# Three small steps of every stage from VectorE to GpSimd, in a scheduled speech-codec encoder

## Chip, cores and metric

The kernel runs on one core of one Trainium2 chip. The metric is the device time of one execution in microseconds (us). Engines are named as in the profile: PE (TensorE), with PEld for its weight loads, DVE (VectorE), ACT (ScalarE), POOL (GpSimd), SP (SyncE, which here only issues DMAs).

## The reference

B = 2, T = 16000, D = 512; three taps, four stages (Nq) of eight codes (C) each; bf16 in and out.

```python
z = silu(sum_i xp[:, i:i+T, :] * dw_enc[i])        # depthwise filter, 3 taps
res, q = z, 0
for s in range(Nq):
    cb = codebooks[s]
    d2 = (res*res).sum(-1)[..., None] - 2 * res @ cb.T + (cb*cb).sum(-1)
    sel = cb[d2.argmin(-1)]
    q, res = q + sel, res - sel
y = sum_i qp[:, i:i+T, :] * dw_dec[i]              # depthwise filter, 3 taps
```

## The kernel before

The 32000 tokens are spread over 128 partitions, 250 positions each. The positions are cut into 16 chunks (`SIZES`: 12, then fourteen of 16, then 14). A chunk lies in SBUF with channels on the partitions, as four column blocks of 128 channels.

**Front of a chunk** (`load`, `front`). SP fetches the rows with transposing DMAs (L486, tile XT, two buffers). For each column block DVE makes three tap products (L553, tiles Z and T). They are added either on DVE (L561) or by an accumulating DMA that POOL issues (L559, Z<-T). The list `DMA_ADDS` says which: all four blocks of the first sum and one block of the second, from the second chunk on. ACT then does exp, log and exp (L565, L573, L576), DVE adds one in between (L569) and multiplies into the residual (L581, tile RES, three buffers).

**A stage** (`stage`, four per chunk). PE multiplies the residual with itself and with the code words into PSUM (L637, L643). DVE takes the diagonal out of it (L651, TR) and copies the dots (L654, PR). Then three small DVE steps over 16 x 8 numbers per partition: `with_norm` adds norm and dots (L673, V), `distance` adds the code norms and writes the upper half of a 32-bit word (L679, KEY), `ranks` writes the lower half (L684), so that ties go to the first code. DVE takes the minimum of the words (L689, M) and compares (L697, OH). PE transposes the one-hot rows (L707), and DVE copies them back (L714, OHT).

For stages 0 to 2 the residual is then updated, one instruction for two quarters of a column block. Either PE selects the code words (L731, SEL) and DVE adds them to RES (L747), or PE also multiplies the old residual by the identity (L752, NEW) and ACT writes the sum back (L758). `ON_DVE` gives the number of the four column blocks that go to DVE in stages 0, 1 and 2; chunk n takes entry n modulo the length, the last three chunks `ON_DVE_LAST`.

**Outputs** (`outputs`, `finish`). PE multiplies the one-hot rows with filtered code words (L785), ACT copies to SBUF (L791), SP stores (L795).

**Order.** All is put in order before the program is built. `Plan` holds a list of tasks with an engine, a hold, a delay and a due time; `run` makes passes forward and backward over it, with random shifts from the seeds in `ROUNDS`; the instructions are then emitted by start time. So each engine runs a fixed queue, with the work of up to three chunks mixed in it. A planned "DMA" engine stands for all DMAs. Its transposes and adds are of two kinds, and `APART` is a gap that the plan puts between kinds.

On the chip `keep_apart` adds a wait: with `LAG` n, each transposing DMA waits for the n-th last add before it in program order, and each add for the n-th last transpose. The adds stand in POOL's queue, transposes and stores in SP's.

Of the kernel before, what the change touches and what calls it, by code (L numbers as in the profile page):

```python
# [13 lines left out]
ALU = mybir.AluOpType  # L14
# [11 lines left out]
SIZES = [12] + [16] * 14 + [14]  # L26


ON_DVE = [(1, 2, 2)]
ON_DVE_LAST = [(2, 2, 2)]  # L30
LAST = 3

# [3 lines left out]

EARLY = 1

RUN = 4

AHEAD = 40
# [2 lines left out]
PERIOD, LEAD, STAGE, LATE, SPREAD = 56, 0.4, 0.9, 0.3, 0.3  # L44
FAR = -3.3e38

ROUNDS = [(940, 0.3, 0.0, 7), (4101, 0.3, 2.0, 9), (5991, 0.3, 0.0, 7), (15520, 0.3, 0.0, 10)]


CELLS, COLUMNS, ROWS = range(3)  # L50
WHOLE = (CELLS, CELLS, 0, 0.0)
SWITCH, CLING, SLOW = 0.1, 10.0, 1.08
RUNS, ADDS = (1, 1, 0, 0.0), (2, 2, 0, 0.0)
APART, CLUMP = 0.5, 2.0

LAG = 2


class Plan:
# [18 lines left out]
    def pass_over(self, rank, backward=False):  # L78

        tasks = self.tasks  # L80
        needs = [t[3] for t in tasks]
        after = [[] for _ in tasks]
        for n, ds in enumerate(needs):
            for d in ds:
                after[d].append(n)
        if backward:
            needs, after = after, needs
        takes, gives = (7, 6) if backward else (6, 7)
        left = [len(d) for d in needs]
        engines = list(dict.fromkeys(t[0] for t in tasks))  # L90
        ready = {e: [] for e in engines}
        until = {e: 0.0 for e in engines}
        slots = dict(self.slots)
        for n, t in enumerate(tasks):
            if not left[n]:
                heapq.heappush(ready[t[0]], (rank[n], n))
        now, events, order, starts, before = 0.0, [], [], [0.0] * len(tasks), WHOLE
        sort, ended = 0, 0.0
        while True:
            going = True  # L100
            while going:
                going = False
                for e in engines:
                    if until[e] > now + 1e-9:
                        continue
                    passed, pick, least, gap = [], None, 0.0, 0.0
                    while e == "DMA" and ready[e]:
                        at, n = heapq.heappop(ready[e])
                        passed.append((at, n))
                        if all(slots[k] > 0 for k in tasks[n][takes]):  # L110
                            kind, lost = tasks[n][8][0], 0.0
                            if kind and sort and kind != sort:
                                lost = max(0.0, APART - (now - ended))
                            if pick is None or at + CLUMP * lost < least:
                                pick, least, gap = n, at + CLUMP * lost, lost
                    while e == "PE" and ready[e]:
                        at, n = heapq.heappop(ready[e])
                        passed.append((at, n))
                        if all(slots[k] > 0 for k in tasks[n][takes]):
                            here = tasks[n][8]  # L120
                            lost = self.between(here, before) if backward else self.between(before, here)
                            if pick is None or at + CLING * lost < least:
                                pick, least, gap = n, at + CLING * lost, lost
                    if pick is not None:
                        passed = [v for v in passed if v[1] != pick]
                        if e == "PE":
                            before = tasks[pick][8]
                        elif tasks[pick][8][0]:
                            sort, ended = tasks[pick][8][0], now + gap + tasks[pick][1]
                    while pick is None and ready[e]:  # L130
                        at, n = heapq.heappop(ready[e])
                        if all(slots[k] > 0 for k in tasks[n][takes]):
                            pick = n
                            break
                        passed.append((at, n))
                    for p in passed:
                        heapq.heappush(ready[e], p)
                    if pick is None:
                        continue
                    t = tasks[pick]  # L140
                    for k in t[takes]:
                        slots[k] -= 1
                    order.append(pick)
                    starts[pick] = now
                    until[e] = now + gap + t[1]
                    heapq.heappush(events, (now + gap + t[1], -1))
                    heapq.heappush(events, (now + gap + max(t[1], t[2]), pick))
                    going = True
            if len(order) == len(tasks):
                return starts, order  # L150
            now = events[0][0]
            while events and events[0][0] <= now + 1e-9:
                _, n = heapq.heappop(events)
                if n < 0:
                    continue
                for k in tasks[n][gives]:
                    slots[k] += 1
                for a in after[n]:
                    left[a] -= 1
                    if not left[a]:  # L160
                        heapq.heappush(ready[tasks[a][0]], (rank[a], a))
# [46 lines left out]
def kernel(  # L208
# [8 lines left out]
    nc = tc.nc  # L217
    P = nc.NUM_PARTITIONS
# [254 lines left out]
    def load(st, org):  # L473
# [10 lines left out]
        def run(n, m):  # L484
            g = g0 + n - 1
            t = nc.sync.dma_start_transpose(out=st["XT"][:, n:n + m, :, :].rearrange("p n i t -> p (n i) t"),  # L486
                                        in_=xv[:, g:g + m, :].rearrange("p g d -> p (g d)"))
            keep_apart(t, runs, adds)
# [26 lines left out]
        for n in range(0, G + 2, RUN):  # L515
            due = org - 2.2 * PERIOD + 0.01 * n
            m = min(RUN, inside - n)
            if m > 0:
                done.append(plan.add("DMA", 0.7 * m, 2.7 + 0.7 * m, [room], due, lambda n=n, m=m: run(n, m), mode=RUNS))
        if inside < G + 2:  # L520
            t = plan.add("DMA", 0.9, 3.2, [room], due, lambda: edge(G + 1), mode=RUNS)
            st["edge"] = plan.add("POOL", 1.0, 1.4, [t], due, lambda: shift(G + 1))
# [91 lines left out]
    def stage(st, s, due):  # L614
# [55 lines left out]

        def with_norm():
            u["V"] = small.tile([P, GC, C], BF16, name="V")
            nc.vector.tensor_tensor(out=u["V"][:, 0:G, :], in0=u["PR"][:, 0:G, :], in1=u["TR"][:, 0:G].to_broadcast([P, G, C]),  # L673
                                    op=ALU.add)

        def distance():
            u["KEY"] = free["KEY"].pop(0)
            g2 = GPOS[:, C * s:C * s + C].rearrange("p (o c) -> p o c", o=1).to_broadcast([P, G, C])
            nc.vector.tensor_tensor(out=u["KEY"][1][:, 0:G, :, 1], in0=u["V"][:, 0:G, :], in1=g2, op=ALU.add)  # L679

        def ranks():

            word = u["KEY"][1]
            nc.vector.scalar_tensor_tensor(out=word[:, 0:G, :, 0], in0=word[:, 0:G, :, 1], scalar=0.0,  # L684
                                           in1=RANK.to_broadcast([P, G, C]), op0=ALU.is_lt, op1=ALU.subtract)

# [28 lines left out]
            st["OHT"] = u["OHT"]  # L715

        due += 0.01 * PERIOD
        t = plan.add("DVE", 0.2, 0.33, maxima, due, with_norm)
        t = plan.add("DVE", 0.2, 0.33, [t] + preset[0:3], due, distance, take=("KEY",))
        t = plan.add("DVE", 0.2, 0.33, [t], due, ranks)  # L720
        t = plan.add("DVE", 0.2, 0.33, [t], due, least)
        t = plan.add("DVE", 0.2, 0.36, [t], due, onehot, take=("OH",) if s == 0 else (), give=("KEY",))
        t = plan.add("PE", 0.056 * MB * SLOW, 0.056 * MB * SLOW + 0.25, [t], due, turn, take=("psA",), give=("OH",) if s == Nq - 1 else ())
# [37 lines left out]
        for j in range(0, J, 2):  # L761
            for i in range(KT):
                if i < on_dve[s]:
                    c = plan.add("PE", 0.08, 0.08 + 0.22 * f * SLOW + 0.2, [t, words], due, lambda i=i, j=j: chosen(i, j), take=("psA",),
                                 mode=(ROWS, ROWS, 3 << j, 0.216 * f * SLOW))
                    st["new"][i, j] = st["new"][i, j + 1] = plan.add("DVE", 0.1 + 1.06 * f, 0.2 + 1.06 * f, [c] + seen, due,
                                                                     lambda i=i, j=j: subtract(i, j), give=("psA",))
                    continue
                c = plan.add("PE", 0.2 + 0.432 * f * SLOW, 0.4 + 0.65 * f * SLOW, [t, words, st["new"][i, j], st["new"][i, j + 1]], due,
                             lambda i=i, j=j: rest(i, j), take=("psA",), mode=(CELLS, ROWS, 3 << j, 0.216 * f * SLOW))  # L770
                st["new"][i, j] = st["new"][i, j + 1] = plan.add("ACT", 0.13 + 0.8 * f, 0.25 + 0.8 * f, [c] + seen, due,
                                                                 lambda i=i, j=j: keep(i, j), give=("psA",))

    kept = {}

# [114 lines left out]
```

## Time and profile before

| | us |
|---|---|
| median of 3 runs | 745.02 (744.42 to 745.52) |
| profiled execution | 742.04 |
| its span on the core | 740.3 |
| DVE busy | 685.9 |
| ACT busy | 665.4 |
| PE busy | 590.8 |
| POOL busy | 81.7 |

Busy time of an engine is a union: instructions that overlap are counted once. The profile's groups give the sum and mean of single durations, which can be more. "Idle before" is time in which the engine had nothing running ahead of that group, and the arrow names what ended it. POOL's busy time before is almost all the issuing of the 75 accumulating DMAs (72.9 us).

### The profile page before, as it was taken

The numbers are of one execution on the slowest core, as the hardware profiler recorded it, in microseconds if no ns is written. First come the engines' busy times: TensorE is split into PE (matmuls) and PEld (weight loads), VectorE is DVE, ScalarE is ACT, GpSimd is POOL, SyncE is SP. The second block draws the span as 40 slices with busy tenths as digits, with TensorE's granted clock in tenths as the row PEclk, the third lists the DMA queues.
The fourth block names the chain that finished last, engine by engine and source line by source line (L and its number), as shares of the span: only waits on it lengthen the run. The fifth ranks groups of instructions, "written<-read, shape, count | busy, mean of one in ns | idle before, by whom it ended". The sixth has DMA issues, their size and how long they took to land. (4 is left out here: it accounts for less than half of the span.)

```text
span 740.3 us, 23586 instructions
## 1 busy us (share of the span) xinstructions
PE 590.8 (80%) x10478; PEld 314.2 (42%) x10544; DVE 685.9 (93%) x1359; ACT 665.4 (90%) x539; POOL 81.7 (11%) x104
## 2 busy tenths in 40 slices
PE   5037687787987888986978888878988898989996
PEld 5023334344444444434444444444453444444543
DVE  6999989899999999997999999989999999998952
ACT  2688979899999999998899999989999999976576
POOL 3112101111101011100101111100111101100000
PEclk9566969999999999999799899999999999999999
DMA  7969795859696967839978875959896435320234
GB/s 178 189 130 182 135 200 104 141 122 201 182 174 158 209 133 164 165 116 143 188 171 177 175 165 143 182 132 174 172 210 136 131 64 152 87 88 2 88 143 199
DMA packets 160833, 111.14 MB, mean 150 GB/s; under 512 B 142426, under 2 KB 142811, under 8 KB 160603
## 3 DMA queue, kind: packets, MB, share of 16 engines
q1 hardware_dynamic: 148976, 69.61, 39.5%
q0 software_dynamic: 11472, 39.76, 29.9%
q8 instruction: 82, 1.34, 0.8%
q10 hardware_dynamic: 282, 0.26, 0.1%
q14 instruction: 21, 0.16, 0.1%
HBM read 2.39 MB, written 32.77 MB: 47 GB/s over the span
## 5 line engine op out<-in xcount | busy, mean ns | idle before, releaser
L758 ACT ACTIVATE RES<-NEW 128x1024 bf16<-128x1024 f32 (+1 forms) x218 | 218.5, 1043 | 28.6 <-PE NEW L731 21.9
L747 DVE TENSOR_TENSOR RES<-RES,SEL 128x1024 bf16<-128x1024 bf16 (+1 forms) x166 | 197.5, 1203 | 6.7 <-PE SEL L731 6.3
L643 PE MATMUL PS<-RES 128*64 128x80 bf16 (+1 forms) x8064 | 176.1, 203 | 11.2 <-DVE RES L581 9.7
L643 PEld LDWEIGHTS <-RES 128*64 128x64 bf16 x8064 | 172.8, 115 | 19.6 <-DVE RES L581 10.6
L752 PE MATMUL NEW<-RES,IDENT 128*128 128x512 bf16 (+1 forms) x436 | 137.7, 399 | 31.3 <-ACT RES L758 15.6
L791 ACT ACTIVATE YSB<-Y 128x1024 bf16<-128x1024 f32 (+1 forms) x126 | 126.6, 1061 | 8.4 <-PE Y L785 4.5
L565 ACT ACTIVATE E<-Z 128x2048 bf16<-128x2048 bf16 (+1 forms) x64 | 123.2, 1931 | 11.5 <-DMA Z<-T 4.0
L559 POOL DMA_DIRECT2D Z<-T x75 | 72.9, 976 | 537.5 <-ACT RES L758 78.8
L573 ACT ACTIVATE LN<-E 128x2048 f32<-128x2048 bf16 (+1 forms) x64 | 123.0, 1923 | 9.9 <-DVE E L569 9.2
L576 ACT ACTIVATE E<-LN 128x2048 bf16<-128x2048 f32 (+1 forms) x64 | 123.0, 1922 | 0.4
L651 DVE TENSOR_REDUCE TR<-PS 128x5 bf16<-128x320 f32 (+1 forms) x188 | 96.0, 515 | 14.4 <-PE PS L643 14.3
L553 DVE TENSOR_SCALAR T<-XT,WENC 128x2048 bf16<-128x2048 bf16 (+1 forms) x128 | 94.8, 745 | 5.1 <-DMA Z<-T 5.1
L731 PEld LDWEIGHTS <-CBN 32*128 32x128 bf16 x768 | 32.6, 92 | 137.7 <-issue 134.3
L785 PE MATMUL Y<-A,OHT 128*128 128x512 bf16 x219 | 77.6, 382 | 16.4 <-ACT RES L758 6.0
L731 PE MATMUL NEW<-OHT,CBN 32*128 32x512 bf16 (+1 forms) x436 | 88.3, 402 | 0.1
L581 DVE TENSOR_TENSOR RES<-Z,E 128x2048 bf16<-128x2048 bf16 (+1 forms) x64 | 77.3, 1208 | 0.0
L731 PE MATMUL SEL<-OHT,CBN 32*128 32x512 bf16 (+1 forms) x332 | 58.7, 396 | 22.0 <-ACT RES L758 13.3
L637 PE MATMUL PS<-MASK,IDENT 128*64 128x320 bf16 (+1 forms) x376 | 64.6, 340 | 8.6 <-DVE PR L654 6.2
L561 DVE TENSOR_TENSOR Z<-Z,T 128x2048 bf16<-128x2048 bf16 (+1 forms) x53 | 62.5, 1181 | 2.7 <-DMA Z<-T 2.7
L752 PEld LDWEIGHTS <-IDENT 128*128 128x128 bf16 x436 | 33.1, 99 | 67.4 <-issue 57.4
L430 PE MATMUL PS<-MASK,IDENT 128*128 128x384 bf16 x167 | 46.2, 359 | 10.1 <-DVE PR L654 9.8
L785 PEld LDWEIGHTS <-OHT 128*128 128x128 bf16 x373 | 32.1, 97 | 50.8 <-issue 22.8
(78 smaller groups left out, 416.2 us busy)
## 6 DMA issues: line engine op xcount, KB each, us to landing
Z<-T POOLq DMA_DIRECT2D x75, 512.0 KB, 5.6
out_dram<-YSB SPq DMA_DIRECT2D x61, 512.0 KB, 3.2
RES<-in_x_dram SPq DMA_DIRECT2D x1, 1664.0 KB, 6.8
XT<-in_x_dram SPq DMA_TRANSPOSE x74, 5.7
out_dram<-YSB SPq DMA_DIRECT2D x1, 384.0 KB, 2.3
out_dram<-YSB SPq DMA_DIRECT2D x1, 256.0 KB, 2.7
A<-in_dw_dec_dram POOLq DMA_DIRECT2D x2, 96.0 KB, 6.4
CB<-in_codebooks_dram ACTq DMA_DIRECT2D x1, 128.0 KB
```

Source lines behind the costliest of these rows:

```text
L553: nc.vector.tensor_scalar(out=places(u[name]), in0=taps(i, k), scalar1=WENC[:, i, k:k + 1], scalar2=None, op0=ALU.mult)
L565: nc.scalar.activation(u["E"][:, 0:G, :], u["Z"][:, 0:G, :], ACT.Exp, scale=-1.0)
L573: nc.scalar.activation(u["LN"][:, 0:G, :], u["E"][:, 0:G, :], ACT.Ln)
L576: nc.scalar.activation(u["E"][:, 0:G, :], u["LN"][:, 0:G, :], ACT.Exp, scale=-1.0)
L643: nc.tensor.matmul(V[h * HT:(h + 1) * HT, r, :], lhsT=half[:, LC:LC + HT], rhs=half[:, lo:hi], start=False, stop=(i == KT - 1), skip_group ...
L651: nc.vector.tensor_reduce(out=u["TR"][:, q:q + m], in_=u["V", q][:, :, own:own + HT], axis=AX.X, op=ALU.max)
L731: nc.tensor.matmul(ps, lhsT=CBN[s][rows, i * P:(i + 1) * P], rhs=u["OHT"][rows, 0:MB, :], start=start, stop=True, skip_group_check=True)
L747: nc.vector.tensor_tensor(out=old, in0=old, in1=u["SEL", i, j][:, :, 0:W].rearrange("p h (m t) -> p h m t", t=HT), op=ALU.add)
L752: nc.tensor.matmul(NEW[:, h, 0:W], lhsT=IDENT, rhs=tokens(i, j + h, 1), start=True, stop=False, skip_group_check=True)
L758: nc.scalar.activation(old, u["NEW", i, j][:, :, 0:W].rearrange("p h (m t) -> p h m t", t=HT), ACT.Copy)
L785: nc.tensor.matmul(Y[:, h, :], lhsT=lhs(), rhs=rhs, start=(a == 0), stop=(a == len(terms) - 1))
L791: nc.scalar.activation(u["YSB"][:, k:k + n, :], u[k][:, 0:n, :], ACT.Copy)
```

## The change

Sum of dots and norm, code norms and rank words go to POOL in all four stages (`ON_POOL`). There the rank step is two instructions instead of one: a compare, then a subtraction. Each of the four waits for the one before. In the plan, the first two have a hold of 0.45 and a delay of 0.65 us, the rank step twice the hold. `LAG` goes from 2 to 1, so each transpose waits for the newest add before it and the reverse; the plan's gaps become 1.9 and 2.3 us, its transposes cost 0.6 us a row in place of 0.7. `ON_DVE` alternates between (2, 2, 2) and (1, 2, 2) in place of (1, 2, 2) throughout. The seeds and passes in `ROUNDS` are others, so the queues of all engines are in a different order.

```diff
-ON_DVE = [(1, 2, 2)]
+ON_DVE = [(2, 2, 2), (1, 2, 2)]
 ON_DVE_LAST = [(2, 2, 2)]
...
+ON_POOL = (0, 1, 2, 3)
+POOL_SMALL = (0.45, 0.65)
...
-ROUNDS = [(940, 0.3, 0.0, 7), (4101, 0.3, 2.0, 9), (5991, 0.3, 0.0, 7), (15520, 0.3, 0.0, 10)]
+ROUNDS = [(802, 2.0, 3.0, 6), (3096, 0.3, 0.0, 8), (3304, 0.3, 0.0, 4), (3638, 1.0, 0.0, 2)]
...
-APART, CLUMP = 0.5, 2.0
-
-LAG = 2
+APART = (0.0, 1.9, 2.3)
+CLUMP = 2.0
+
+LAG = 1
...
-                                lost = max(0.0, APART - (now - ended))
+                                lost = max(0.0, APART[sort if backward else kind] - (now - ended))
...
-                done.append(plan.add("DMA", 0.7 * m, 2.7 + 0.7 * m, [room], due, lambda n=n, m=m: run(n, m), mode=RUNS))
+                done.append(plan.add("DMA", 0.6 * m, 2.4 + 0.6 * m, [room], due, lambda n=n, m=m: run(n, m), mode=RUNS))
...
-            nc.vector.tensor_tensor(out=u["V"][:, 0:G, :], in0=u["PR"][:, 0:G, :], in1=u["TR"][:, 0:G].to_broadcast([P, G, C]),
+            small_on(s).tensor_tensor(out=u["V"][:, 0:G, :], in0=u["PR"][:, 0:G, :], in1=u["TR"][:, 0:G].to_broadcast([P, G, C]),
                                     op=ALU.add)
...
-            nc.vector.tensor_tensor(out=u["KEY"][1][:, 0:G, :, 1], in0=u["V"][:, 0:G, :], in1=g2, op=ALU.add)
+            small_on(s).tensor_tensor(out=u["KEY"][1][:, 0:G, :, 1], in0=u["V"][:, 0:G, :], in1=g2, op=ALU.add)
...
             word = u["KEY"][1]
+            if s in ON_POOL:
+                nc.gpsimd.tensor_scalar(out=u["V"][:, 0:G, :], in0=word[:, 0:G, :, 1], scalar1=0.0, scalar2=None, op0=ALU.is_lt)
+                nc.gpsimd.tensor_tensor(out=word[:, 0:G, :, 0], in0=u["V"][:, 0:G, :], in1=RANK.to_broadcast([P, G, C]), op=ALU.subtract)
+                return
...
-        t = plan.add("DVE", 0.2, 0.33, maxima, due, with_norm)
-        t = plan.add("DVE", 0.2, 0.33, [t] + preset[0:3], due, distance, take=("KEY",))
-        t = plan.add("DVE", 0.2, 0.33, [t], due, ranks)
+        e, a, b = ("POOL",) + POOL_SMALL if s in ON_POOL else ("DVE", 0.2, 0.33)
+        t = plan.add(e, a, b, maxima, due, with_norm)
+        t = plan.add(e, a, b, [t] + preset[0:3], due, distance, take=("KEY",))
+        t = plan.add(e, 2 * a if s in ON_POOL else a, a + b if s in ON_POOL else b, [t], due, ranks)
...
+    def small_on(s):
+        return nc.gpsimd if s in ON_POOL else nc.vector
```

## The prediction

> **What bounds the kernel now.** I read the page first: the shares of the engines and the slices of the span.
>
> ```profile
> span 740.3 us, 23586 instructions
> PE 590.8 (80%) x10478; PEld 314.2 (42%) x10544; DVE 685.9 (93%) x1359; ACT 665.4 (90%) x539; POOL 81.7 (11%) x104
> ...
> DVE  6999989899999999997999999989999999998952
> ACT  2688979899999999998899999989999999976576
> ```
>
> No single engine carries the whole span. There is a start-up, a long middle in which DVE and ACT are both full, and an end in which both thin out. The table by stretches says how full:
>
> ```profile
> 100.00:660.00 560.00, 470.51 (x8652) 248.58 (x8709) 542.66 (x1068) 541.70 (x437) 61.55 (x67) 0.96 0.74 154
> 660.00:740.00 80.00, 69.19 (x1177) 35.26 (x1178) 52.02 (x112) 52.19 (x55) 0.00 (x0) 0.99 0.27 107
> ```
>
> The columns are length, then busy us of PE, PE's weight load, DVE, ACT, POOL, then granted clock, DMA share, GB/s. In the middle DVE is busy 542.66 of 560 us and ACT 541.70: 97% each. To win there, both must be relieved. In the last 80 us DVE and ACT are at 65%: there the length of the chain through a stage counts.
>
> Third, the groups of the lines that the change touches, and the only POOL rows near to what it adds:
>
> ```profile
> L758 ACT ACTIVATE RES<-NEW 128x1024 bf16<-128x1024 f32 (+1 forms) x218 | 218.5, 1043 | 28.6 <-PE NEW L731 21.9
> L747 DVE TENSOR_TENSOR RES<-RES,SEL 128x1024 bf16<-128x1024 bf16 (+1 forms) x166 | 197.5, 1203 | 6.7 <-PE SEL L731 6.3
> L679 DVE TENSOR_TENSOR KEY<-V,GPOS 128x128 bf16<-128x128 bf16 (+1 forms) x64 | 19.3, 302 | 0.2
> L496 POOL COPY XT<-XE 128x508 bf16<-128x508 bf16 x1 | 0.6, 610 | 13.4 <-DMA XE<-in_x_dram 13.4
> masks.py:199 POOL TENSOR_SCALAR_AFFINE_SELECT IDENT<-IDENT 128x128 bf16<-128x128 bf16 x1 | 0.3, 283 | 0.0
> ```
>
> Last, the timelines of DVE and POOL side by side, where a POOL instruction runs beside large DVE ones (start, duration):
>
> ```profile
> 585.53 1.28 POOL L559 DMA_DIRECT2D Z<-T  x1 [11.14 <-ACT LN L573]
> 585.97 0.76 DVE L553 TENSOR_SCALAR T<-XT,WENC 128x2048 bf16<-128x2048 bf16 x1
> ...
> 556.75 0.61 POOL L496 COPY XT<-XE 128x508 bf16<-128x508 bf16 x1 [13.38 <-DMA XE<-in_x_dram]
> 557.01 1.43 DVE L581 TENSOR_TENSOR RES<-Z,E 128x2048 bf16<-128x2048 bf16 x1
> ```
>
> The add's issue on POOL takes 0.86 us in most rows. Here it took 1.28 and ended at 586.81, 0.08 us after the product at L553. The second pair is the other direction: L581 has a median of 1.22 us, and 1.43 was the longest of its 64. It started inside POOL's copy. So the two engines hold each other up at SBUF, both ways.
>
> **Part 1, three steps off DVE.** V (L673), KEY (L679) and the rank words (L684) leave DVE: 192 instructions with means of 289 to 302 ns. But neighbours on DVE overlap: between other work such a step takes 0.20 us from its start to the next one's (L679 starts at 302.58, the next at 302.79). In the middle 53 stages lie: 53 x 3 x 0.20 = 31.8 us less DVE.
>
> **Part 2, updates from ACT to DVE.** Even chunks below the last three update two column blocks in stage 0 instead of one: 7 chunks x 2 halves = 14 updates. On DVE each takes 1.13 us start to start (324.71 to 325.84): +15.8. On ACT 0.92 start to start: -12.9. PE loses 28 identity matmuls (L752), about 0.2 us each; PE has 80% and I count nothing.
>
> **Part 3, four steps on POOL.** The rank step becomes two, so 256 instructions over 128 elements per partition. No row has a POOL step with two inputs. The lower bound is the one-input select over 128 elements, 0.28 us; the upper is the 508-element copy, 0.61. Two-element copies (L504) take 0.17, so a copy's slope is (610 - 174)/506 = 0.86 ns per element. A second input read at that slope makes 0.17 + 2 x 0.11 = 0.39. I take 0.39 for the three with two inputs and 0.28 for the compare: 1.45 us, 0.36 in the mean. Two dependent copies at L508 (180 ns each) span 0.42, a gap of 0.06; five gaps make 0.30. The bare chain is 1.75 us, where the last stage on DVE now takes 1.00 (725.75 to 726.75). The Trainium skill (GPSIMD Engine Reference, 3.1 Elementwise) gives two-input steps about 2.6 cycles per element at 1.2 GHz; as an estimate from that page 128 elements are 0.28 us before dispatch, so with 0.17 of dispatch 0.45, and the sum below would rise by about 5 us (part 4 goes with the square of the length, 13 to 17, and each chain of part 7 grows by 0.18).
>
> **Part 4, what the shared access costs DVE.** The DVE groups that could collide are those with two inputs in SBUF or shown to block POOL: L553, L569, L581, L561, L697. In the middle they are 149 + 52 + 53 + 39 + 54 = 347 starts (0.62 per us) and 276 busy us, 49%. 53 x 4 = 212 POOL steps fall there. If they fall at random, each meets 0.62 x 0.36 = 0.22 starts and delays them by half its length: 212 x 0.22 x 0.18 = 8.4 us. If every POOL step lies just before the next DVE instruction, and that is a colliding one in 38% of cases (347 of about 920 left), 212 x 0.38 x 0.36 = 29. Zero if POOL always gives way. I take 13, nearer to random. The skill (SBUF - State Buffer, Who interferes with whom) says that whoever starts first holds the shared port pair for its whole instruction and the other blocks fully. The two pairs of rows above agree.
>
> **Part 5, the new wait.** DVE's minimum (L689) now waits for POOL; behind it in DVE's queue stands all other DVE work, and PE's transposes wait for what follows. In the changed program's instruction order I summed, stage by stage, the DVE work between the last copy of dots (L654) and the minimum, with the mean of each row less 0.1 us of overlap: median 3.1 us, a quarter under 2.7. Against it stands the POOL chain: 1.75 bare, plus port waits. A step meets a held port in 49% of cases and waits the mean rest of it, 0.45 us (sum of squares over twice the sum of those five groups): 4 x 0.22 = 0.9. That is 2.6 us: most stages are covered, some not. I take 0.15 us per stage, 8 us in all. The ends are 0 (always covered) and 53 x (4.95 - 3.1) = 98, if each POOL step waited out 0.8 us.
>
> **Part 6, transposes and adds.** With LAG 1 each group waits for the newest of the other kind. From the trace's packet records up to 660 us: transposes active 210 us, adds 260, both 44, neither 234. A transposing packet took 32.0 ns beside adds and 22.8 alone. Serial, the 44 us become about 70, so 26 more, inside 234 us without either. Direction changes in program order go from 57 to 61. I count 0; if the cover fails, up to 26. The add issues stand on POOL's queue, now in front of stage steps; that is rival C.
>
> **Part 7, the end.** Seven stages lie after 660, with nothing to fill their DVE queue. About four of them follow one another in the last chunk. Each chain grows by 0.75 (0.4 to 1.7 by the bounds of part 3): +3 us (1.7 to 7).
>
> **Sum.** Middle, DVE: -31.8 + 15.8 + 13 + 8 = +5. ACT: -12.9, so DVE sets it again. End: +3. Together +8 on the profiled execution of 742.04 us (span 740.3): 750.0. The median of the runs is 745.02, 2.98 higher; the same +8 gives 753.0.
>
> **The rivals.** B, faster: POOL's steps slip between DVE's and the minimum finds its words ready. Then DVE has -16 and ACT -12.9; ACT decides, 12.9 x 560/541.7 = -13, and +3 at the end: 735. For it: POOL is busy 11%, the one collision seen cost 0.21 us, and the cover exceeds the bare chain in nearly every middle stage. Against: 49% of DVE's time collides. It decides while port cost and waits together stay under 13 us. Chance 0.36.
>
> C, much slower: POOL's queue is in order, and in the changed order 41 of the 64 stage chains stand directly behind an add's issue, 20 behind two. An issue takes 0.86 us and waits first for its product, its buffer and, with LAG 1, the newest transposes; POOL spent 537 us waiting before such issues, which harmed nobody while only adds stood there. Half of 41 x 0.86 = 35 on DVE is 18 more: 771; with longer waits 785. It decides once an add is late by more than the slack of about 0.5 us that part 5 leaves. Chance 0.17.
>
> D, the work moves as said and the terms cancel within 0.2% (1.5 us, about what a measurement here can tell from no change): 0.06. That the change doesn't do what it says is excluded by the order: 192 steps are gone from DVE and 256 are on POOL.
>
> **How the numbers follow.** Forecast (745 + 1.5 to 763) 0.41; B 0.36, and the forecast's own lower spread adds 0.01 to faster; C 0.17; D 0.06. I say faster 0.37, same 0.06, slower 0.57. The forecast's own range is 747 to 763. The range to hold 8 in 10 reaches from B's 735, less 2 for a cheaper end, to 774, past C's middle: 733 to 774.
>
> **What would show it.** After: V and KEY steps on POOL at 0.35 to 0.5 us, some near 1; L581 and L561 with more rows above 1.3 us; DVE's wait before the minimum, released by POOL, between 5 and 15 us; ACT's busy time down by about 13; the stretch after the last front work 3 us longer. Wrong for B: DVE idles under 3 us at the minimum and busy falls by 16. Wrong for C: POOL's steps wait for adds, and DVE's idle at the minimum is over 20 us.

## The result, and the profile after

The changed kernel takes 767.21 us (median of 4 runs, 765.34 to 770.84) against 745.27 (the kernel before, 4 runs): a ratio of 1.029, 95% interval 1.025 to 1.034. The forecast was 753. The sign was right, the size was not: +22 us in place of +8. The profiled execution took 770.84 us, with a span of 769.1, which is 28.8 more than before. That is 6.9 more than the medians lie apart: the profiled execution is the slowest of the four here, and the one before was 3 us under its median.

The page of the changed kernel, the same lines as before:

```profile
span 769.1 us, 23664 instructions
PE 611.6 (80%) x10520; PEld 321.4 (42%) x10520; DVE 673.7 (88%) x1181; ACT 657.0 (85%) x525; POOL 244.9 (32%) x360
...
DVE  5989999799999999989988979989899899977851
ACT  2688798698989988989989997989999799986576
```

DVE works 12.2 us less than before (673.7 against 685.9) and yet its span is 28.8 longer, so it idles 41.0 us more: 95.4 in place of 54.4. ACT works 8.4 us less. Several 9s in both rows of slices have become 8s. The table by stretches (columns as before) shows where:

```profile
0.00:100.00 100.00, 49.51 (x657) 29.14 (x658) 87.02 (x165) 67.17 (x46) 30.14 (x50) 0.69 0.76 148
100.00:690.00 590.00, 492.91 (x8786) 258.26 (x8784) 541.70 (x932) 535.67 (x424) 203.03 (x284) 0.92 0.69 148
690.00:769.00 79.00, 69.22 (x1080) 33.95 (x1078) 44.98 (x85) 54.12 (x57) 11.71 (x27) 0.99 0.29 115
```

The middle holds the same 542 us of DVE work as before and takes 590 us for it in place of 560. DVE is no longer full there (92%). The end is 79 us long in place of 80, but it is cut by hand where DVE thins out, so this says little. The granted clock in the middle is 0.92 in place of 0.96. What DVE waits for, by the list of waits (total us, times, longest), first before, then after:

```profile
DVE TR L651 <- PE PS L643: 14.3, 14, 3.4
...
DVE T L553 <- DMA Z<-T: 5.1, 4, 4.2
DVE OHT L714 <- PE ps_oh L707: 5.0, 7, 2.0
DVE Z L561 <- DMA Z<-T: 2.7, 2, 2.5
```

```profile
DVE M L697 <- POOL KEY L690: 28.5, 29, 4.2
DVE TR L655 <- PE PS L647: 16.9, 23, 4.1
DVE OHT L722 <- PE ps_oh L715: 8.3, 13, 2.1
...
DVE Z L565 <- DMA Z<-T: 7.5, 6, 2.8
```

The first line after is new: the minimum waits for the words from POOL, 28.5 of the 41.0 us. Of these, 21.1 lie in the middle (53 stages), 3.1 before it and 4.2 in the end (7 stages). The other 12.5 are for the most part small increases of waits that were there, 8.7 of them for PE (31.8 before, 40.5 after).

This is the account of DVE; it doesn't show that DVE alone sets the time. ACT's idle time grew by 37.2 us as well (74.9 to 112.1), about three quarters of it in waits for PE. And after the first 100 us the clock was granted at half for 96.5 us in place of 42.9. Each of these stretches but the last, at the very end, followed 3.4 us in which PE had been busy 0 to 73%, against 85% in the mean, so the lower clock looks like a consequence of PE's waits that then adds to them. No run holds the clock fixed, so its share isn't known.

The groups of the four POOL steps (count, busy us, mean ns), and one stretch in which they are held up, from the timelines of POOL and of DVE:

```profile
L677 POOL TENSOR_TENSOR V<-PR,TR 128x128 bf16<-128x128 bf16 x60 | 45.1, 751 | 261.3 <-DVE PR L658 261.2
L689 POOL TENSOR_SCALAR V<-KEY 128x128 bf16<-128x128 bf16 x60 | 42.6, 711 | 4.9
L683 POOL TENSOR_TENSOR KEY<-V,GPOS 128x128 bf16<-128x128 bf16 x60 | 36.8, 613 | 4.5
L690 POOL TENSOR_TENSOR KEY<-V,RANK 128x128 bf16<-128x128 bf16 x60 | 32.6, 544 | 5.0
```

```profile
316.86 0.40 POOL L677 TENSOR_TENSOR V<-PR,TR 128x128 bf16<-128x128 bf16 x1 [9.44 <-DVE PR L658]
317.34 0.83 POOL L683 TENSOR_TENSOR KEY<-V,GPOS 128x128 bf16<-128x128 bf16 x1
318.25 0.84 POOL L689 TENSOR_SCALAR V<-KEY 128x128 bf16<-128x128 bf16 x1
319.18 0.85 POOL L690 TENSOR_TENSOR KEY<-V,RANK 128x128 bf16<-128x128 bf16 x1
```

```profile
317.16 0.75 DVE L557 TENSOR_SCALAR T<-XT,WENC 128x2048 bf16<-128x2048 bf16 x1
...
317.93 0.78 DVE L557 TENSOR_SCALAR T<-XT,WENC 128x2048 bf16<-128x2048 bf16 x1
...
319.03 0.74 DVE L557 TENSOR_SCALAR T<-XT,WENC 128x2048 bf16<-128x2048 bf16 x1
```

The first step runs free and takes 0.40 us. Each of the next three starts beside a tap product and takes 0.83 to 0.85. The step at 317.34 ends at 318.17, 0.26 after the product that held it (317.16 + 0.75 = 317.91). So here a step that starts beside such an instruction is done only after it.

The longest chains have another reason. POOL's queue also holds the issues of the adds, and one can stand between two steps (POOL, then DVE):

```profile
390.05 0.39 POOL L677 TENSOR_TENSOR V<-PR,TR 128x128 bf16<-128x128 bf16 x1 [5.45 <-DVE PR L658]
395.10 0.87 POOL L563 DMA_DIRECT2D Z<-T  x1 [4.66 <-DMA XT<-in_x_dram]
395.69 0.71 POOL L683 TENSOR_TENSOR KEY<-V,GPOS 128x128 bf16<-128x128 bf16 x1
```

```profile
397.53 0.29 DVE L697 TENSOR_REDUCE M<-KEY 128x16 f32<-128x128 f32 x1 [3.32 <-POOL KEY L690]
```

The add waited 4.66 us for a transpose, its turn under LAG 1, and the second step stood behind it. In 13 of the 64 stages an add's issue ran between the last dots' copy and the last of the four steps, and 16.1 of the 28.5 us of waiting belong to these 13. By the length of the gaps in those chains about 13 of the 16.1 are due to the adds; this is an estimate.

### The profile page after: what moved, and what is told of

Its sections match the earlier page's. It is cut to its first block, busy times and chain, and to the rows that moved or that the text cites. A ratio compares the mean times of both kernels' runs of the same rounds, so it can differ in the third digit from the quotient of the medians.

```text
span 769.1 us, 23664 instructions
## 1 busy us (share of the span) xinstructions
PE 611.6 (80%) x10520; PEld 321.4 (42%) x10520; DVE 673.7 (88%) x1181; ACT 657.0 (85%) x525; POOL 244.9 (32%) x360
## 4 chain that ended last, share of the span: by engine, by line
DVE 27%; PE 17%; ACT 9%; DMA 7%; POOL 6%; issue 4%; SPq 2%; ACTq 0%; POOLq 0%; DVEq 0%
DVE RES L756 11%; PE PS L647 5%; PE Y L797 4%; DMA Z<-T 3%; DVE TR L655 3%; DVE T L557 3%; DMA XT<-in_x_dram 3%; PE NEW L761 3%; ACT RES L767 3%; DVE Z L565 2%; ACT LN L577 2%; ACT YSB L803 2%; PE NEW L740 2%; DVE RES L585 2%; DVE E L573 2%
## 5 line engine op out<-in xcount | busy, mean ns | idle before, releaser
L767 ACT ACTIVATE RES<-NEW 128x1024 bf16<-128x1024 f32 (+1 forms) x204 | 202.8, 1020 | 40.5 <-PE NEW L740 31.3
L756 DVE TENSOR_TENSOR RES<-RES,SEL 128x1024 bf16<-128x1024 bf16 (+1 forms) x180 | 212.1, 1194 | 7.5 <-PE SEL L740 7.0
L647 PE MATMUL PS<-RES 128*64 128x80 bf16 (+1 forms) x8064 | 184.0, 206 | 9.9 <-DVE RES L585 7.5
L647 PEld LDWEIGHTS <-RES 128*64 128x64 bf16 x8064 | 180.4, 118 | 18.9 <-DVE RES L585 8.3
L761 PE MATMUL NEW<-RES,IDENT 128*128 128x512 bf16 (+1 forms) x408 | 132.7, 409 | 23.1 <-DVE RES L756 10.8
L677 POOL TENSOR_TENSOR V<-PR,TR 128x128 bf16<-128x128 bf16 (+1 forms) x64 | 50.6, 791 | 276.9 <-DVE PR L658 276.8
L569 ACT ACTIVATE E<-Z 128x2048 bf16<-128x2048 bf16 (+1 forms) x64 | 121.1, 1892 | 16.0 <-DVE Z L565 13.4
L577 ACT ACTIVATE LN<-E 128x2048 f32<-128x2048 bf16 (+1 forms) x64 | 121.4, 1896 | 13.6 <-DVE E L573 13.5
L655 DVE TENSOR_REDUCE TR<-PS 128x5 bf16<-128x320 f32 (+1 forms) x188 | 94.8, 509 | 17.3 <-PE PS L647 16.9
L797 PE MATMUL Y<-A,OHT 128*128 128x512 bf16 x249 | 87.9, 401 | 15.1 <-DVE RES L756 5.0
L557 DVE TENSOR_SCALAR T<-XT,WENC 128x2048 bf16<-128x2048 bf16 (+1 forms) x128 | 95.2, 756 | 0.6 <-DMA Z<-T 0.6
L740 PE MATMUL SEL<-OHT,CBN 32*128 32x512 bf16 (+1 forms) x360 | 66.8, 401 | 26.3 <-ACT RES L767 9.3
L740 PE MATMUL NEW<-OHT,CBN 32*128 32x512 bf16 (+1 forms) x408 | 83.7, 407 | 0.2 <-DVE OHT L722 0.2
L585 DVE TENSOR_TENSOR RES<-Z,E 128x2048 bf16<-128x2048 bf16 (+1 forms) x64 | 77.3, 1207 | 1.4 <-ACT E L580 1.0
L565 DVE TENSOR_TENSOR Z<-Z,T 128x2048 bf16<-128x2048 bf16 (+1 forms) x53 | 63.3, 1197 | 7.5 <-DMA Z<-T 7.5
L434 PE MATMUL PS<-MASK,IDENT 128*128 128x384 bf16 x171 | 53.5, 398 | 11.0 <-DVE PR L658 11.0
```

Of the source, the lines that this page charges most:

```text
L557: nc.vector.tensor_scalar(out=places(u[name]), in0=taps(i, k), scalar1=WENC[:, i, k:k + 1], scalar2=None, op0=ALU.mult)
L569: nc.scalar.activation(u["E"][:, 0:G, :], u["Z"][:, 0:G, :], ACT.Exp, scale=-1.0)
L577: nc.scalar.activation(u["LN"][:, 0:G, :], u["E"][:, 0:G, :], ACT.Ln)
L647: nc.tensor.matmul(V[h * HT:(h + 1) * HT, r, :], lhsT=half[:, LC:LC + HT], rhs=half[:, lo:hi], start=False, stop=(i == KT - 1), skip_group ...
L655: nc.vector.tensor_reduce(out=u["TR"][:, q:q + m], in_=u["V", q][:, :, own:own + HT], axis=AX.X, op=ALU.max)
L740: nc.tensor.matmul(ps, lhsT=CBN[s][rows, i * P:(i + 1) * P], rhs=u["OHT"][rows, 0:MB, :], start=start, stop=True, skip_group_check=True)
```

## The experiments

All ratios below are to the kernel before, run beside it, with their 95% intervals. The expectations name three explanations: theory P (POOL's chain of four steps brings the words too late, so DVE idles), rival L (the strict turns of transposes and adds under LAG 1 delay the adds and POOL's queue behind them) and rival O (the new order of the queues is worse by itself).

### One part at a time, in a fixed order

Five runs each leave the order of the queues as it was in one of the two kernels. First only the steps on POOL, in the old order, with the old waits:

```diff
-            nc.vector.tensor_tensor(out=u["V"]...         # likewise KEY; the ranks as a compare and a subtraction
+            nc.gpsimd.tensor_tensor(out=u["V"]...
```

> The kernel before, its order and its waits, but the three small steps of every stage emitted on POOL (four instructions there). DVE is relieved of about 38 us, ACT of nothing, so no large gain is possible. Theory P: POOL's chain of about 3.2 us eats what DVE has between the dots' copy and the minimum; DVE idles 15 to 30 us before the minimum and the time is 748 to 760 us. Rival L: the old waits are in place, so 742 to 747. Rival O: 742 to 747, for the order is the old one.

Measured: 755.33 us, 1.016 (1.013 to 1.019), within theory P's range and over that of the rivals. DVE is relieved of 29 us (656.9 busy) and waits 31.3 us for POOL, by its list of waits:

```profile
DVE M L689 <- POOL KEY L685: 31.3, 32, 3.7
```

So the move by itself costs 11.6 us, with no other part of the change, in an order that was planned for steps on DVE. Here an add's issue is in the way in 26 stages, and they have 17.7 of the 31.3 us. Now only the turns of the DMAs, in the old order:

```diff
-LAG = 2
+LAG = 1
```

> The kernel before with LAG 1 in place of 2: same queues, stricter waits between transposes and adds, all small steps still on DVE. Theory P: the strict turns cost little, 745 to 749 us. Rival L: 755 to 768. Rival O: 745 to 749.

Measured: 785.07 us, 1.057 (1.053 to 1.062), more than rival L said and far over theory P's 745 to 749. Here the adds come late, above all for the sums on DVE (and 10.4 us for products):

```profile
DVE Z L561 <- DMA Z<-T: 26.9, 15, 4.1
```

The old order was planned with a gap of 0.5 us between kinds; strict turns cost it 41 us. The same switch in the new order, which was made for gaps of about 2 us:

```diff
-LAG = 1
+LAG = 2
```

> The changed kernel with LAG 2 in place of 1: all queues in the same order, only the waits between transposes and adds are the old, looser ones. Theory P (DVE idles because POOL's four steps, held up by DVE's own instructions, bring the words too late for the minimum): nothing there changes, 764 to 769 us, and DVE's wait before the minimum stays at 25 to 30 us. Rival L (the strict turns of transposes and adds delay the adds, and POOL's queue behind them): 748 to 756, and SP's wait for adds falls from 290 us to about 100. Rival O (the new order of the queues is worse by itself): 764 to 769.

Measured: 765.29 us, 1.031 (1.025 to 1.036), the same as the change within the intervals. The turns are looser on SP's queue, as its list of waits shows (the change, then this run), and the time doesn't follow:

```profile
SPq L490 <- DMA Z<-T: 289.8, 29, 19.5
```

```profile
SPq L490 <- DMA Z<-T: 167.2, 20, 16.0
```

DVE's wait for POOL fell from 28.5 to 21.0 us, below the 25 to 30 that theory P gave, and the part of it in stages with an add's issue in the way from 16.1 to 7.0. So strict turns did hold up POOL's steps, as rival L said; but in the new order taking this away didn't shorten the kernel by anything that shows. Last, the new order with the small steps back on DVE, with LAG 1 and with LAG 2:

```diff
-        return nc.gpsimd if s in ON_POOL else nc.vector
+        return nc.vector                              # and the fused rank step
```

> The changed kernel's own order of all queues, LAG 1, but the small steps emitted on DVE in their places (three instructions there, the rank words fused as before). DVE gets 38.6 us of work back. Theory P (POOL's chain late for the minimum costs about as much as the relief of DVE is worth): the 28.5 us of waiting go and 38.6 us of work come, 765 to 777 us. Rival O (this order is bad whoever does the steps; DVE's other idle time of about 67 us stays): 775 to 785. If POOL were the whole loss, the time would be that of before, 745 to 752.

> As the kernel with the small steps back on DVE in the changed order, but LAG 2: what is left of the change is the order and 14 updates more on DVE. Rival L (strict turns of transposes and adds hurt where DVE is late): 8 to 40 us faster than with LAG 1. Theory P: within 5 us of LAG 1. DVE carries 712 us of work in it, so nothing under 750 is expected.

Measured: 772.00 us, 1.039 (1.033 to 1.046), and 773.40, 1.041 (1.035 to 1.047). The first is within theory P's 765 to 777 and under rival O's 775 to 785, and the second within 5 us of it, as P said for LAG. In the new order POOL saves about 5 us, with intervals that just touch: it takes 32.6 us off DVE (706.3 against 673.7 busy) and gives 28.5 back as waiting. The order with 14 more updates on DVE is slow without POOL too.

### What makes POOL's chain long

Here the old order and LAG 2 again, with one step on POOL, with two, and with all four over one row of 16 (8 elements per partition in place of 128), first row and last row. The last two leave out the other 15 rows, so they don't compute the function; they only show what the length of a step does.

> The kernel before, its order and waits, with only the first of the three steps (norm plus dots) on POOL. DVE is relieved of 13 us. Theory P (the loss is the length of POOL's chain against the DVE work that stands between): one step of 0.4 us bare and 0.75 with what DVE holds up is covered nearly everywhere; DVE waits under 10 us for it and the time is 741 to 748 us. If any handing over to POOL cost the same, whatever the chain's length: 750 to 757, as with four steps.

> The kernel before, its order and waits, with the first two steps (norm plus dots, code norms) on POOL and the rank words on DVE. Theory P: chain about 1.5 us, DVE waits 8 to 20 us for it, time 743 to 751 us, between one step and four. If the loss did not go with the chain's length: 750 to 757.

> The kernel before with all four steps on POOL, but each over one row of the 16 (8 elements per partition; the other rows of the words stay constant, so that part of the distances is left out). If what makes POOL's chain long is being held up by DVE's instructions, it stays over 2.2 us, DVE waits over 18 us and the time is 749 to 756 us, near the 755 of the full steps. If it is POOL's own work per element, the chain falls to about 1.2 us, the wait under 8 us and the time to 738 to 746.

> As the run with one row of 16 in the old order, but the last row in place of the first (the other rows are left out), so that the first step waits for the last dots' copy as the full step does. Theory P as amended: the wait goes with the whole length of the chain, bare work and holding up together; with steps of 0.2 us bare the chain is about 1.7 us in place of 3.4, DVE waits 6 to 14 us before the minimum, and the time is 740 to 748 us. If DVE's holding up alone made the wait: over 20 us and 750 to 756.

Measured:

| on POOL | us | ratio | DVE busy | DVE's wait for POOL | of it with an add's issue in the way |
|---|---|---|---|---|---|
| nothing | 742.6 to 746.7 | 1 | 685.9 | 0 | 0 |
| one step | 747.35 | 1.006 (1.003 to 1.010) | 676.7 | 4.9 | 0 |
| two steps | 748.17 | 1.007 (1.003 to 1.010) | 665.7 | 14.1 | 2.0 |
| four | 755.33 | 1.016 (1.013 to 1.019) | 656.9 | 31.3 | 17.7 |
| four, first row only | 742.25 | 0.996 (0.992 to 1.001) | 651.9 | 7.7 | 7.0 |
| four, last row only | 739.23 | 0.990 (0.985 to 0.994) | 651.6 | 11.1 | 7.5 |

The last column is the wait in those stages where an add's issue ran between the last dots' copy and the last step. The wait goes with the chain's length, as theory P said, and a longer chain also meets more adds. The run with the first row doesn't separate the causes: its first step may start before the last dots are copied. The run with the last row has no such head start, and the steps are still held up in it:

```profile
L674 POOL TENSOR_TENSOR V<-PR,TR 128x8 bf16<-128x8 bf16 x64 | 35.9, 560 | 227.1 <-DVE PR L655 227.0
L680 POOL TENSOR_TENSOR KEY<-V,GPOS 128x8 bf16<-128x8 bf16 x64 | 25.9, 405 | 4.3
L685 POOL TENSOR_SCALAR V<-KEY 128x8 bf16<-128x8 bf16 x64 | 24.2, 378 | 5.0
L686 POOL TENSOR_TENSOR KEY<-V,RANK 128x8 bf16<-128x8 bf16 x64 | 17.7, 277 | 5.3
```

Bare they take 0.19 to 0.23 us, their shortest rows. Taking away the work per element leaves 11.1 of 31.3 us, though the holding up by DVE goes on, and most of these 11.1 belong to stages with an add in the way. No run takes the holding up or the adds away, so their shares are not measured one by one. Relieving DVE by 9 us with a wait of only 4.9 (one step) gained nothing: ACT has 666 us busy in all these runs, and DVE's waits for PE grew instead (19.8 us before L651 with one step, 14.3 without). So a saving on DVE's account isn't yet a saving of time.

The same in the new order:

> The changed kernel in its own order, with the rank words back on DVE as one instruction and two steps left on POOL. DVE gets 13 us of work back. Theory P: DVE's wait for POOL falls from 28.5 us to 10 to 18, which about pays for it, 760 to 769 us. Rival O: 767 to 777, since the order has no room for 13 us more on DVE.

> The changed kernel in its own order with LAG 1, each of the four POOL steps over the last row of 16 only (the other rows are left out). Theory P: the chain halves, DVE waits under 12 us before the minimum in place of 28.5 and the time falls by 12 to 20, to 747 to 756 us. Rival O (order and turns hold the rest): 757 to 766 with the same short wait.

Measured: with two steps 768.45 us, 1.031 (1.024 to 1.037); with four over the last row 758.79 us, 1.022 (1.013 to 1.031). The wait falls to 16.6 and to 13.6 us; of the 13.6, 12.0 belong to 27 stages with an add in the way. Neither run decides between theory P and rival O. With two steps the time lies in both ranges. With the short steps the four runs spread from 749.94 to 766.20 us, over both; their median is 8 us under the change, while P expected 12 to 20, and the intervals overlap.

### The order

These runs plan the queues again, which changes everything at once, so each tells only about a kind of order. First the planner is told about what a POOL step takes here; then the change without POOL, with the seeds left as they are and with seeds chosen anew (here and below by the plan's own end, which is no measured time):

```diff
-POOL_SMALL = (0.45, 0.65)
+POOL_SMALL = (0.72, 0.82)                             # and ROUNDS chosen anew
```

> The changed kernel, with the planner told that a POOL step holds 0.72 and delays 0.82 us (the means on the chip with what DVE holds up) in place of 0.45 and 0.65, and with seeds chosen anew for that plan. The minimum then stands about 0.8 us later behind the dots. Theory P: DVE's wait before the minimum falls from 28.5 us to under 15 and the time to 748 to 760. Rival O or L: 762 to 772 whatever the wait does.

> The changed kernel with no stage on POOL and one update less on DVE in even chunks, so the split of work is that of before; LAG 1, the new gaps, costs and seeds stay, and the queues are planned again. Theory P: with the POOL chain gone the time is near that of before, 742 to 752 us. Rival L: 758 to 768, as the strict turns are still there. Rival O: anything up to 768, since these seeds give the order.

> No stage on POOL and the split of before, as in the run planned again without POOL, LAG 1 and the new gaps, but with seeds chosen anew for that plan. Theory P: strict turns that the plan knows of cost little, 743 to 755. Rival L: 765 to 785, as in the kernel before with LAG 1. If it is far under the 789 of the run with the seeds left as they were, the seeds made most of that.

Measured: 787.89 us, 1.061 (1.055 to 1.067), with the wait still 29.4 us (24.0 of it in 22 stages with an add in the way), so that expectation missed entirely; 788.95, 1.063 (1.059 to 1.067), over every expectation; and 766.52, 1.031 (1.025 to 1.038), in rival L's range. The last has the old split of work, nothing on POOL, and is as slow as the change. So I ran fresh orders of the kernel before, of the change, and of the change with the old gaps and LAG 2:

> The kernel before with only its seeds chosen anew by the planner's own end: same work, LAG 2, old gaps, another order of the queues. Rival O (the time hangs on which order it is, and that of before is a good one among those that plan equally): 755 to 775 us. Rival L (the new gaps and LAG 1 made the slow orders): 742 to 752.

> As the first run with new seeds for the kernel before, with a second, independent choice of seeds. Rival O: 755 to 775 us, and a difference of some us from the first. Rival L: 742 to 752.

> The changed kernel with only its seeds chosen anew by the planner's own end. Rival O: its own order is an ordinary one, so 757 to 785 us. Rival L: 762 to 772, as the strict turns set it. Theory P adds to both the wait of DVE for POOL, 20 to 32 us before the minimum.

> The change without its part on DMA: four steps on POOL and more updates on DVE, but LAG 2, the old gap of 0.5 us and the old cost of transposes, with seeds chosen anew for that plan. Rival L: 738 to 752. Theory P: 752 to 765, with 20 to 32 us of waiting before the minimum. Rival O: anywhere from 750 to 785.

Measured: 757.60 us, 1.020 (1.012 to 1.028), and 753.47, 1.015 (1.008 to 1.022), for the kernel before with other `ROUNDS` alone; 772.28, 1.039 (1.031 to 1.046), with POOL and the old turns. The runs of the change's fresh order lie too far apart for a time (774 to 881 us), so only the wait before the minimum is read: 36.3 us, where 20 to 32 were expected. So an order alone is worth 13 to 17 us: that is what the kernel before has over two others for the same work (740.70 beside them). The first lies in rival O's range, the second between the two. With POOL and the old turns the time lies over both L's 752 and P's 765, in O's range, which was 35 us wide; the wait for POOL there, 18.5 us in the slowest of its executions, is under P's 20 to 32. None of the runs that compute the whole points to a version that beats both kernels.

## Why the prediction was right or wrong

**Part 1 held.** Taking the steps off DVE is worth 32.6 us of busy time between the two runs in the new order. That is net of the 4.3 us in part 4; the two together, 36.9, compare with 64 x 3 x 0.20 = 38.4 for all stages (31.8 was said for the middle).

**Part 2 was a little short for DVE.** DVE's balance is -12.2: the 32.6 less, and 20.4 more for the updates in their new order (706.3 with the steps on DVE against 685.9 before), where 15.8 was said. ACT lost 8.4 by union in place of 12.9.

**Part 3 was short by the compare.** Free steps over 128 elements take 0.39, 0.40, 0.52 and 0.40 us, in sum 1.72 (1.45 was said). The 0.39 for the steps with two inputs was right. The compare, with one input, is the longest of the four, not the shortest as I took it. The bare chain in the end stretch is 1.98 us, not 1.75.

**Part 4 had the wrong payer.** 13 us were put on DVE. The large DVE groups that collide grew by 12 ns (L557 into T, x120), 27 ns (into Z, x60), 20 ns (L565, x45), 6 ns (L573, x60) and 0 (L585): 4.3 us in all. POOL pays instead: of its 256 steps 93 had one of those four lines running 0.1 us after their start, and became 0.40 to 0.91 us longer in the mean, about 57 us (47 x 0.46 + 19 x 0.91 + 15 x 0.90 + 12 x 0.40). The rows behind this part had hinted at it: in the first pair POOL's instruction had started first (585.53 against 585.97), and still it was the one that ran longer. So the two pairs did not both agree with the rule that whoever starts first holds the other.

**Part 5 is the step that failed.** I took 8 us of waiting in the middle; it was 21.1 there, and 28.5 in all. In the middle the chain took 3.2 us in the mean, up to 7.45, where 2.6 was said. Part 5 put the adds' issues in POOL's queue at nothing; I had set them apart as rival C, with a chance of 0.17. The 13 stages in which one was in the way all lie in the middle, with 16.1 us of waiting. The other 40 stages there have 5.0 us, less than the 8 that part 5 took for bare steps and holding up alone, and their chain is 2.9 us in the mean. The way to the 8 was weak besides: I compared a mean chain with a median cover and then took 0.15 us a stage by eye. Both spread by microseconds, and a wait is made of the bad tail: five stages, each with an add in the way, have 13.4 of the 21.1 us, though half of the stages had the minimum within 0.06 us of the words' arrival.

**Part 6 held for its zero, with another meaning.** LAG alone is worth nothing that shows in the new order's time, though 7.5 us of DVE's wait for POOL, and 41 us in the old. The separate price, slower orders, was not in the sum.

**Part 7 had the chain right in size.** At the end it is 1.98 us in place of 1.00, and DVE waited 4.2 us for POOL there. The end stretch didn't become longer (79 us in place of 80, where 3 more were said), but its cut is by hand.

**The sum left out a term.** I carried the old order's other idle time over to the new one. It grew by 12.5 us. What an order is worth was not in the sum at all, and the fresh orders of the old kernel (13 and 17 us) show that it is larger than the whole forecast of 8. In the sum's own terms the +8 was -3 of DVE's work (-31.8 + 15.8 + 13), 8 of waiting and 3 at the end; the 28.8 measured on the span are -12.2 of work, 28.5 of waiting for POOL and 12.5 of other idle time. So the work came out 9 us better than forecast, and the idle time 30 us worse. The sign was right partly by luck: the new order is as slow with the steps on DVE.

**Rival B** failed where it said it would: port cost and waits came to 33 us, far over 13. **Rival C** had the mechanism that part 5 lacked: stage steps that stand in POOL's queue behind an add, which in the two longest cases waited for the newest transposes. It was at work in 13 stages, not in 41, and mostly between the steps; the first step started only 0.23 us after the last dots' copy in the mean (up to 3.14). The 16.1 us there are near the 18 that C added, and the time is near its 771. But this isn't the whole loss: with looser turns that part fell to 7.0 us, and the time stayed.

How the 22 us divide is only partly settled. In the old order the move to POOL is 11.6 us, and it turns into a gain of 0.4% (within the noise) or 1% if the steps are cut to one row. In the new order shortening them may recover about 8 of 22, which its four runs don't establish. The rest goes with the order, with its wider gaps and 14 more updates on DVE. Whether these orders are slow because of the gaps (with nothing on POOL and the new gaps 1.031 and 1.063, with the old gaps 1.015 and 1.020) or by the luck of the seeds stays open, as there are only two orders of each kind.

## What to carry to other kernels

Work moved off a full engine helps only if its result is back before that engine asks for it: sum the stretch between, and weigh the spread of both sides, not their middles. Look at what else stands in the helping engine's queue: here the stages with a DMA issue in the way, 13 of 64, had over half of the waiting. A step on an engine that shares memory access with a full one must be priced with the full one running; the bare chain from an idle stretch was 1.98 us, under two thirds of the 3.2 in the middle. And where a planner fixes the queues, a change that plans anew has the worth of the order as a term of its own: measure it by planning the unchanged kernel again.

## What the runs showed of the hardware

DVE and POOL at SBUF held each other up very unequally. In the changed kernel a POOL step that started beside L557, L573, L585 or L565 came out longer by 0.46, 0.40, 0.91 and 0.90 us in the mean, nearly the rest of the DVE instruction (0.49, 0.40, 0.95, 0.98). Beside L756, whose second input is in PSUM, 81 steps came out longer by 0.03 us, and beside the reduction L655, which reads PSUM, 24 by at most 0.02. DVE's own instructions grew by at most 27 ns in the mean. In the other order of starts, 17 instructions of these four lines started while a POOL step that had begun free had 0.23 us of its bare time left in the mean; they came out 0.06 us longer. So in this trace starting first did not let POOL hold DVE for the rest of its step. The Trainium skill (SBUF - State Buffer, Who interferes with whom) names these classes: two-port forms and two SBUF inputs collide, one SBUF input outside those forms and reductions don't. This case's trace agrees in each class, if L557 and L573 (tensor_scalar) ran in such a form, which it doesn't show.
